# Sums of two passes transposed in 32x32 squares by VectorE in place of TensorE, with 256-byte stores

## The chip, the core and the metric

The kernel runs on one core of a Trainium2 chip. The metric is device time in microseconds (us) from start to end of one execution; lower is better. The core has TensorE (matmuls and, in the profile's own row PEld, its weight loads), VectorE (DVE), ScalarE (ACT), GpSimd (POOL) and SyncE (SP, which here issues nearly all DMAs). Sixteen DMA engines move data between DRAM and the on-chip memory SBUF; matmul results land in PSUM.

## The reference

Three layers follow each other: a linear attention over 4 batches, 8 heads, 576 positions of 64 numbers, normalised by its root mean square, which gives 2304 rows of 512; a feed-forward layer; and a mixture of four experts, all of them applied to all rows. Everything is float32:

```
kv = einsum('bhsd,bhse->bhde', k, v);  o = einsum('bhsd,bhde->bhse', q, kv)
x = (o / sqrt(mean(o * o, -1) + 1e-06) * g_norm)      # as 2304 x 512
h = x @ w_in                                          # 512 x 2048
x = (h * clip(h + 3, 0, 6) / 6) @ w_out               # 2048 x 512
p = domain_probs / (domain_probs.sum(-1) + 1e-09)     # 2304 x 4
for e in range(4):                                    # w1[e] 512 x 1024, w2[e] 1024 x 512
    out += p[:, e:e + 1] * (maximum(x @ w1[e], 0) @ w2[e])
```

Output row b*576 + s*9 + j belongs to batch b and to position (s, j) of its sequence, s from 0 to 63 and j from 0 to 8.

## The kernel before

All products are in f32 split in a high and a low part (three matmuls each). The first layer keeps its activations transposed (features on partitions, rows on the free axis); so do the experts.

The experts run in three passes of 768 rows. A pass has eight groups (g), each of two blocks of 256 hidden features; a two-by-two scheme with seven products in place of eight is used for both matrices. `front` makes the seven first products of a block (`product`, line 932, into the PSUM banks qa and qb); it reads the combined first weights `win`, two buffers, each loaded from DRAM by `load_win` (line 967) when the block two before it is done (line 1045). `back` (line 1068) makes one of the seven second products of a group in a PSUM slot (sx, sy, sz) from the combined second weights `tt` (loaded by `feed`, line 974, into four buffers, and into four more that `room` adds at the end of group 7) and adds it into the pass's sums: `acc2[th, c]`, two tiles of 128 output columns by 384 rows for each half of the rows (th) and of the 512 columns (c). VectorE does these additions (line 901) and the elementwise work of `front` and `prep`.

The sums are transposed, so a pass ends with `flush` (line 914), called four times for each of the first two passes: three times in the pass's last group (lines 1141 and 1142, after steps 2, 5 and 6), once in step 0 of the next group (line 1144). A flush makes six TensorE transposes of 128x128 into a PSUM slot, two ScalarE copies into `done` tiles in SBUF, and six stores (`store`, line 903), each of 64 rows and 256 columns, 1 KB a row. The third pass ends otherwise: its sums are transposed into PSUM with the last products (line 1169), copied to SBUF by VectorE (line 1193) and ScalarE (line 1191), and stored in rows of 2 KB from SyncE's and ScalarE's queues.

The second weights are made earlier, during the first layer, by `blocks(k, 1)` (line 667): each block of raw weights (rawt) is combined and split into high and low parts by VectorE (lines 701 and 688) and ScalarE (line 687) and written to DRAM (`dtw`, and `dwo` for the last group). A column half of 256 is contiguous there.

Order: the first stage is written out by hand; from the first layer on, a planner orders the instructions of each engine by its own costs, and each engine then runs its queue strictly in that order. SyncE's queue holds the loads of tt and win, the broadcast probabilities and the stores.

Of the kernel before, what the change touches and what calls it, by code (L numbers as in the profile page):

```python
# [11 lines left out]
AF = mybir.ActivationFunctionType  # L12
# [5 lines left out]
def kernel(  # L18
# [18 lines left out]
    nc = tc.nc  # L37
    B, H, S, D = q.shape
    NT, DM = out.shape
    E = moe2_w1.shape[0]  # L40
    P = 128
# [6 lines left out]
    CJ = S // CP  # L48
    CB = TB // CP
    HH = H // 2  # L50
# [39 lines left out]
    NG = CJ * 2  # L90
# [10 lines left out]
    ident = const.tile([P, P], F32, name="ident")  # L101
# [110 lines left out]
    half = [slice(x * D, (x + 1) * D) for x in range(2)]  # L212
# [243 lines left out]
    last = {}  # L456
# [5 lines left out]
    done = [False]  # L462
# [54 lines left out]
    with tc.manual_schedule(engines=engines):  # L517
# [88 lines left out]
        for kind, t in (("o", 1), ("i", 3), ("o", 2), ("i", 4), ("o", 3), ("o", 4)):  # L606
# [6 lines left out]
            if t == 2:  # L613
                for y in range(2):
                    nc.sync.dma_start(
                        out=dp[half[y]], in_=moe2_domain_probs.rearrange("(b s j) e -> s b j e", b=B, j=CJ))
# [4 lines left out]
        for y in range(2):  # L621
            h = half[y]
            for jp in range(2):
                j = slice(2 * y + jp, CJ - 1, 4)
                nc.vector.tensor_tensor(
                    out=prob[h, :B * HH].rearrange("p (b a) e -> p b a e", b=B)[:, :, 2 * jp:2 * jp + 2],
                    in0=dp[h, :, j], in1=psum_e[h, :, j].unsqueeze(3).to_broadcast([D, B, 2, E]), op=ALU.mult)
            nc.vector.tensor_tensor(
                out=prob[h, B * HH:], in0=dp[h, y::2, CJ - 1],
                in1=psum_e[h, y::2, CJ - 1:].to_broadcast([D, 2, E]), op=ALU.mult)  # L630

    TC = DM // 2
    experts = [(e, j) for e in range(E) for j in range(FP)]
    NG = len(experts) // 2
    INPASS = [3, 5, 7, 9, 11, 13]
# [28 lines left out]

    turns = [0]

    def blocks(k, h):

        r = rawt[k, h]
        last = k - 2 * NG + 2 if h else -1  # L670

        def new():
            turns[0] += 1
            z = ring[turns[0] % len(ring)]
            if not isinstance(z, str):
                return z
            return cvp.tile([P, 2, TC], F32R, tag=z, bufs=2 if z == "r" else 1, name="tb")

        def keep(m, src, low, n=2):
            high = new()  # L680
            low = low if low is not None else new()
            hi, lo = high[:, :n], low[:, :n]
            if src is None:
                src = lo.bitcast(F32)
            elif not h:
                hi, lo = (x.rearrange("p m (c f) -> p (m c) f", c=2) for x in (hi, lo))
            nc.scalar.activation(out=hi, in_=src, func=AF.Copy)
            nc.vector.tensor_tensor(out=lo, in0=src, in1=hi.bitcast(F32), op=ALU.subtract)
            for y, x in ((0, high), (1, low)):
                if not h:  # L690
                    nc.sync.dma_start(
                        out=dwin[k][:, y, m:m + n].rearrange("p m c f -> p m (c f)"), in_=x[:, :n].bitcast(F32))
                    continue
                c = min(n, 7 - m) if m else 1
                nc.sync.dma_start(out=dtw[k // 2][:, m:m + c, k % 2, y], in_=x[:, :c].bitcast(F32))
                if last >= 0 and m < 2:
                    nc.sync.dma_start(
                        out=dwo[last][:, int(m > 0), y].rearrange("p (c d) -> p c d", c=2), in_=x.bitcast(F32))

        def sub(out, a, b, op=ALU.subtract):  # L700
            nc.vector.tensor_tensor(out=out, in0=a, in1=b, op=op)

        odd = new()
        od = odd.bitcast(F32)
        if h:
            sub(od, r[:, 1::2], r[:, 0:2])
        else:
            q = r.rearrange("p c (i f) -> p i c f", i=2)
            a11, a12, a21, a22 = (q[:, i, 2 * c:2 * c + 2] for i in range(2) for c in range(2))
            o4 = od.rearrange("p m (c f) -> p m c f", c=2)  # L710
            sub(o4[:, 0], a21, a22, ALU.add)
            sub(o4[:, 1], o4[:, 0], a11)
        yield
        even = new()
        ev = even.bitcast(F32)
        if h:
            sub(ev[:, 0], r[:, 3], od[:, 0])
            sub(ev[:, 1], r[:, 2], ev[:, 0])
        else:
            e4 = ev.rearrange("p m (c f) -> p m c f", c=2)  # L720
            sub(e4[:, 0], a11, a21)
            sub(e4[:, 1], a12, o4[:, 1])
        yield
        keep(3, None, odd)
        yield
        keep(5, None, even)
        yield
        if h:
            keep(1, r[:, 2:4], None)
        else:  # L730
            keep(0, q[:, 0], None)
        yield
        if not h:
            keep(2, a22, None, 1)
        elif last >= 0:
            keep(0, r[:, 0:2], None)
        else:
            keep(0, r[:, 0:1], None, 1)
        rawt.pop((k, h))
        load_rawt()  # L740
        yield
# [47 lines left out]
    NPASS = len(PASSES)  # L789
    NG2 = NPASS * NG  # L790

    rows = [[(BLK[k][0] + o + y) // P for h in ps for k, o, ln, _ in h for y in range(0, ln, P)] for ps in PASSES]
# [94 lines left out]
    def slot_tile(name):  # L887
        z = slots[0] % 10
        slots[0] += 1
        return (gp if z < 8 else rp).tile([P, TB], F32, tag=("gH", "gL")[z % 2] if z < 8 else "r", name=name)  # L890
# [9 lines left out]
            else:  # L900
                nc.vector.tensor_tensor(out=a, in0=ps[:, d, :TH], in1=a, op=ALU.add)  # L901

    def store(n, src, cols, last=False):
        for y in range(2):
            if n < B * HH:
                b, a = divmod(n, HH)
                j = 4 * (a % 2) + a // 2 + 2 * y
            else:
                b, j = 2 * (n - B * HH) + y, CJ - 1
            queue = nc.scalar if y and last else nc.sync  # L910
            queue.dma_start(
                out=out.rearrange("(b s j) d -> b j s d", b=B, j=CJ)[b, j][:, cols], in_=src[half[y]])

    def flush(p, th, c, slot):

        part = acc2.pop((th, c))
        for i in range(3):
            for d in range(2):
                nc.tensor.transpose(  # L919
                    slot[:, i // 2, ((i % 2) * 2 + d) * P:((i % 2) * 2 + d + 1) * P], part[d][:, i * P:(i + 1) * P], ident)  # L920
        for i0, n in ((0, 2), (2, 1)):
            t = slot_tile("done")
            nc.scalar.activation(out=t[:, :n * TC], in_=slot[:, i0 // 2, :n * TC], func=AF.Copy)
            for i in range(n):
                store(rows[p][3 * th + i0 + i], t[:, i * TC:(i + 1) * TC], slice(c * TC, (c + 1) * TC))

    def product(k, bank, m, first):
        n = 0
# [192 lines left out]
    for g in range(NG2 - 1):  # L1121
        nxt = ahead + front(g + 1, 1)
        if (g + 2) % NG == 0 and g + 2 < NG2:
            b = build((g + 2) // NG)
            bld = {2: "5-", 4: "6-", 7: 1, 9: 6, 10: 2, 12: 5, 13: "7-", 15: 7, 16: 3, 17: "4-", 18: 4}
        else:
            bld = {z - 14: m for z, m in bld.items() if z > 13}
        ci = convert_in(2 * g + 3, *halves) if 2 * g + 3 in INPASS else iter(())
        for s in range(7):
            if s < 5:  # L1130
                prep(g, s + 2)
            back(g, s)
            for z in BEHIND[s]:
                nxt[z]()
                if z in bld:
                    b[bld[z]]()
                if z % 2:
                    next(ci, None)
            if g % 2 and s == 3:
                load_probs(g // 2 + 2)  # L1140
            if g % NG == NG - 1 and s in (2, 5, 6):
                flush(g // NG, *((0, 0), (1, 1), (1, 0))[s - 4 if s > 4 else 0], sz if s == 6 else sx)
            if g % NG == 0 and g and s == 0:
                flush(g // NG - 1, 0, 1, sz)
            if s == 5 and g + 1 < NG2 - 1:
                prep(g + 1, 0)
        if g == NG - 1:
            for _ in range(2):
                room(accp, "acc", 2)
        if g + 1 < NG2 - 1:  # L1150
            ahead = front(g + 2, 0)
            ahead[0]()
            prep(g + 1, 1)

    g = NG2 - 1
# [20 lines left out]
    for z, (jj, i, f) in enumerate(order):  # L1176
        if i not in [w[1] for w in order[:z]]:
            turn_back(i)
        last = i not in [w[1] for w in order[z + 1:]]
        t, o = divmod(i * P, TH)  # L1180
        for m, (sy_, ty) in enumerate(((0, 0), (0, 1), (1, 0))):
            nc.tensor.matmul(  # L1182
                ps[i], lhsT=hs[t, f][:, sy_, jj, o:o + P], rhs=wl[jj][:, f, ty],
                start=False, stop=last and m == 2, skip_group_check=True)
        if not last:
            continue
        r = slot_tile("done")
        for y in range(2):
            cols = slice(y * TC, (y + 1) * TC)
            if y:  # L1190
                nc.scalar.activation(out=r[:, cols], in_=ps[i][:, cols], func=AF.Copy)
            else:
                nc.vector.tensor_copy(out=r[:, cols], in_=ps[i][:, cols])
        store(rows[NPASS - 1][i], r, slice(0, DM), True)


# [28 lines left out]
```

## Time and profile before

| | |
|---|---|
| median of 3 runs | 1172.46 us (1172.0 to 1173.09) |
| profiled execution | 1172.47 us, span 1170.7 us, granted clock 0.999 |
| TensorE busy | 1157.8 us (99%) |
| VectorE busy | 914.8 us (78%) |
| ScalarE busy | 515.2 us (44%) |
| flush, TensorE transposes | 48, 6.5 us busy in all |
| flush, ScalarE copies | 16 |
| flush, stores | 48 of 64 KB, on SyncE's queue |

Busy time is the time in which an engine worked on an instruction; the span is the time from the first to the last instruction. The DMA share is the mean busy share of the sixteen DMA engines. A DMA row's duration is what SyncE spent to issue it; landing is when the data had arrived.

### The profile page before, as it was taken

How to read it: one execution, taken by the hardware profiler on the slowest of the kernel's cores; microseconds unless marked ns; L12 is line 12 of the kernel's file. 1: busy time of each engine (PE TensorE's matmuls, PEld its weight loads, DVE VectorE, ACT ScalarE, POOL GpSimd, SP SyncE). 2: the span in 40 equal slices, each digit the busy share in tenths (PEclk: the TensorE clock that was granted, in tenths of full speed). 3: DMA queues.
4: the chain of work that ended last, by engine and by line, in shares of the span. 5: the costliest groups of instructions: out<-in, count | busy, mean ns of one | idle time of the engine just before them, and what ended most of it. 6: DMA issues, size and time to landing. Idle time of an engine off the chain costs nothing.

```text
span 1170.7 us, 19129 instructions
## 1 busy us (share of the span) xinstructions
PE 1157.8 (99%) x7351; PEld 1082.2 (92%) x7351; DVE 914.8 (78%) x1602; ACT 515.2 (44%) x907; POOL 7.6 (1%) x15
## 2 busy tenths in 40 slices
PE   8999999999999999999999999999999999999998
PEld 6788888888888889999999999999999999999996
DVE  5889999977897854788888896777778867777773
ACT  6877555644555532433333444333334443333321
POOL 1100000000000000000000000000000000000000
PEclk9999999999999999999999999999999999999999
DMA  8723267488599552587878789777777887777821
GB/s 313 248 76 115 87 229 282 137 272 262 179 345 379 211 193 94 201 286 272 283 273 295 271 301 327 262 261 268 253 268 252 282 299 273 252 266 252 289 80 54
DMA packets 117219, 279.24 MB, mean 239 GB/s; under 512 B 10176, under 2 KB 69640, under 8 KB 110728
## 3 DMA queue, kind: packets, MB, share of 16 engines
q1 hardware_dynamic: 116644, 277.24, 69.1%
q8 instruction: 58, 0.95, 0.3%
q10 hardware_dynamic: 484, 0.79, 0.2%
q14 instruction: 33, 0.27, 0.1%
HBM read 212.41 MB, written 65.57 MB: 237 GB/s over the span
## 4 chain that ended last, share of the span: by engine, by line
PE 93%; DVE 3%; DMA 2%; ACT 1%; issue 0%; ACTq 0%; SPq 0%; DVEq 0%
PE slot L1078 29%; PE po L402 16%; PE qa L932 15%; PE qb L932 15%; PE ph L367 5%; PE ph L368 5%; PE ph L369 5%; PE slot L1182 1%; DMA kin<-in_k_dram 1%; DMA vin<-in_v_dram 1%; DMA qin<-in_q_dram 1%; DVE xl L323 1%; PE slot L919 0%; PE kvp L254 0%; PE zp L500 0%
## 5 line engine op out<-in xcount | busy, mean ns | idle before, releaser
L1078 PE MATMUL slot<-so,tt 128*128 128x384 f32 x1932 | 362.2, 334 | 0.0
L1078 PEld LDWEIGHTS slot<-so,tt 128*128 128x128 f32 x1932 | 337.0, 188 | 0.0
L932 PE MATMUL qa<-xs,win 128*128 128x384 f32 x1008 | 202.7, 335 | 0.2 <-ACT qa L1016 0.2
L932 PE MATMUL qb<-xs,win 128*128 128x384 f32 x1008 | 201.9, 334 | 0.0
L402 PE MATMUL po<-gH,w 128*128 128x512 f32 (+1 forms) x632 | 191.0, 368 | 0.2 <-ACT gH L383 0.2
L901 DVE TENSOR_TENSOR acc<-slot,acc 128x384 f32<-128x384 f32 x252 | 128.6, 551 | 63.3 <-PE slot L1078 63.1
L932 PEld LDWEIGHTS qa<-xs,win 128*128 128x128 f32 x1008 | 176.9, 188 | 0.9 <-ACT qa L1016 0.5
L932 PEld LDWEIGHTS qb<-xs,win 128*128 128x128 f32 x1008 | 176.9, 188 | 0.3 <-DVE ar L1011 0.2
L813 ACT ACTIVATE so<-ar 128x768 fp32r<-128x768 f32 x142 | 119.4, 844 | 99.3 <-PE slot L1078 52.9
L814 DVE TENSOR_TENSOR so<-ar,so 128x768 fp32r<-128x768 f32 x142 | 133.9, 953 | 25.8 <-ACT so L813 24.6
L402 PEld LDWEIGHTS po<-gH,w 128*128 128x128 f32 x632 | 115.6, 188 | 20.4 <-ACT gH L383 0.6
L367 PE MATMUL ph<-xh,w 128*128 128x512 f32 (+1 forms) x320 | 118.6, 371 | 0.1
L368 PE MATMUL ph<-xl,w 128*128 128x512 f32 (+1 forms) x320 | 117.9, 368 | 0.0
L369 PE MATMUL ph<-xh,w 128*128 128x512 f32 (+1 forms) x320 | 117.8, 368 | 0.0
L402 PE MATMUL po<-gL,w 128*128 128x512 f32 (+1 forms) x316 | 116.4, 368 | 0.0
L380 ACT ACTIVATE r<-ph,three 128x512 f32<-128x512 f32 (+1 forms) x80 | 51.1, 639 | 57.2 <-PE ph L369 56.4
L381 DVE SCALAR_TENSOR_TENSOR r<-r,ph 128x512 f32<-128x512 f32 (+1 forms) x80 | 50.4, 630 | 30.1 <-ACT r L380 29.7
L367 PEld LDWEIGHTS ph<-xh,w 128*128 128x128 f32 x320 | 60.3, 188 | 10.9 <-DVE r L381 0.5
L369 PEld LDWEIGHTS ph<-xh,w 128*128 128x128 f32 x320 | 60.3, 188 | 10.0
L368 PEld LDWEIGHTS ph<-xl,w 128*128 128x128 f32 x320 | 60.3, 188 | 9.9
L402 PEld LDWEIGHTS po<-gL,w 128*128 128x128 f32 x316 | 59.6, 189 | 9.9 <-DVE gL L384 0.2
L1058 DVE TENSOR_TENSOR ar<-ar 128x768 f32<-128x768 f32 x69 | 65.7, 952 | 0.6
(173 smaller groups left out, 1181.4 us busy)
## 6 DMA issues: line engine op xcount, KB each, us to landing
tt<-dtw SPq DMA_DIRECT2D x161, 512.0 KB, 4.8
win<-dwin SPq DMA_DIRECT2D x40, 1792.0 KB, 7.7
dtw<-tb SPq DMA_DIRECT2D x74, 256.0 KB, 4.9
dwin<-win SPq DMA_DIRECT2D x8, 1792.0 KB, 9.2
rawt<-in_moe_w_dram SPq DMA_DIRECT2D x24, 512.0 KB, 4.5
dwin<-tb SPq DMA_DIRECT2D x38, 256.0 KB, 3.4
raw<-in_moe_w_in_dram SPq DMA_DIRECT2D x14, 512.0 KB, 3.8
raw<-in_moe_w_out_dram SPq DMA_DIRECT2D x14, 512.0 KB, 3.5
```

The costliest lines, as they stand in the source:

```text
L367: nc.tensor.matmul(ph, lhsT=w[:, 0, c, :], rhs=xH[t][:, c, :], start=(c == 0), stop=False)
L368: nc.tensor.matmul(ph, lhsT=w[:, 0, c, :], rhs=xL[t][:, c, :], start=False, stop=False)
L369: nc.tensor.matmul(ph, lhsT=w[:, 1, c, :], rhs=xH[t][:, c, :], start=False, stop=(c == KD - 1))
L380: lambda: nc.scalar.activation(out=r, in_=ph, func=AF.Relu, bias=three[:, 0:1]),
L381: lambda: nc.vector.scalar_tensor_tensor(out=r, in0=r, scalar=6.0, in1=ph, op0=ALU.min, op1=ALU.mult),
L402: nc.tensor.matmul(po_t[u, t][o], lhsT=lhsT, rhs=rhs, start=(f == 0 and m == 0), stop=(f == UF[u] - 1 and m == 2))
L813: nc.scalar.activation(out=dst[0], in_=src, func=AF.Copy)
L814: nc.vector.tensor_tensor(out=dst[1], in0=src, in1=dst[0].bitcast(F32), op=ALU.subtract)
L901: nc.vector.tensor_tensor(out=a, in0=ps[:, d, :TH], in1=a, op=ALU.add)
L932: nc.tensor.matmul(bank, lhsT=w[:, wy, AOP[m], c], rhs=xs[m][:, xy, c], start=first and n == 0, stop=n == 5, skip_group_check=True)
L1058: nc.vector.tensor_tensor(out=dst, in0=a, in1=b, op=op)
L1078: nc.tensor.matmul(slot[:, d, :TH], lhsT=t[:, jj, ty, d * P:(d + 1) * P], rhs=o[:, sy_, jj], start=fresh and m == 0, stop=m == 5, skip_gro ...
```

## The change

The order of the second weights' output columns is changed: within a half of 256, the even columns come first, then the odd ones (`apart`, and the rearranged raw tile in `blocks`). So the two tiles of `acc2[th, c]` hold the even and the odd columns. `flush` lets VectorE transpose each tile in 32x32 squares into a `done` tile and puts even and odd results side by side: then a partition holds, for each of its output rows, 64 neighbouring columns, 256 bytes. A store takes 32 rows by 256 columns from all 128 partitions, so a flush has twelve stores in place of six, all on SyncE's queue. The last pass's copies put even and odd columns back in their places.

```diff
     def blocks(k, h):
         r = rawt[k, h]
+        if h:
+            r = r.rearrange("p c (m d) -> p c d m", d=2)
...
+            if h and src.shape[-1] == P:
+                hi, lo = apart(hi), apart(lo)
...
-            sub(od, r[:, 1::2], r[:, 0:2])
+            sub(apart(od), r[:, 1::2], r[:, 0:2])
...
-    def flush(p, th, c, slot):
+    def flush(p, th, c):
 
         part = acc2.pop((th, c))
-        for i in range(3):
+        for i0, n in ((0, 2), (2, 1)):
+            t = slot_tile("done").rearrange("p (b j d) -> p b j d", d=2, j=QP)
             for d in range(2):
-                nc.tensor.transpose(
-                    slot[:, i // 2, ((i % 2) * 2 + d) * P:((i % 2) * 2 + d + 1) * P], part[d][:, i * P:(i + 1) * P], ident)
-        for i0, n in ((0, 2), (2, 1)):
-            t = slot_tile("done")
-            nc.scalar.activation(out=t[:, :n * TC], in_=slot[:, i0 // 2, :n * TC], func=AF.Copy)
+                nc.vector.transpose(
+                    out=t[:, :n * P // QP, :, d],
+                    in_=part[d][:, i0 * P:(i0 + n) * P].rearrange("p (b j) -> p b j", j=QP))
             for i in range(n):
-                store(rows[p][3 * th + i0 + i], t[:, i * TC:(i + 1) * TC], slice(c * TC, (c + 1) * TC))
+                m = rows[p][3 * th + i0 + i]
+                for y in range(2):
+                    for z in range(2):
+                        nc.sync.dma_start(
+                            out=place(m, y)[z * QP:(z + 1) * QP, c * TC:(c + 1) * TC].rearrange(
+                                "i (a f) -> a i f", a=P // QP),
+                            in_=t[:, 4 * i + 2 * y + z].rearrange("p j d -> p (j d)"))
...
+            o = r[:, cols].rearrange("p (m d) -> p d m", d=2)
+            z = ps[i][:, cols].rearrange("p (d m) -> p d m", d=2)
             if y:
-                nc.scalar.activation(out=r[:, cols], in_=ps[i][:, cols], func=AF.Copy)
+                nc.scalar.activation(out=o, in_=z, func=AF.Copy)
             else:
-                nc.vector.tensor_copy(out=r[:, cols], in_=ps[i][:, cols])
+                nc.vector.tensor_copy(out=o, in_=z)
```

`QP` is 32, `P` 128, `TC` 256. `place(n, y)` gives the 64 output rows of half y of tile n, as `store` computed them before.

## Rows read from the trace of the kernel before

**Rows 1.** Page, part 1: busy us, share of the span, instructions of each engine.
```profile
PE 1157.8 (99%) x7351; PEld 1082.2 (92%) x7351; DVE 914.8 (78%) x1602; ACT 515.2 (44%) x907; POOL 7.6 (1%) x15
```

**Rows 2.** Busy time by stretch (us, engines, clock, DMA share, GB/s).
```profile
684.00:700.00 16.00, 16.00 (x96) 15.97 (x95) 15.42 (x28) 4.78 (x8) 0.00 (x0) 1.00 0.91 303
700.00:712.00 12.00, 12.00 (x78) 11.90 (x77) 9.67 (x14) 6.52 (x13) 0.00 (x0) 1.00 0.83 282
...
230.00:395.00 165.00, 165.00 (x774) 138.40 (x773) 133.90 (x250) 86.31 (x155) 0.00 (x0) 1.00 0.86 291
```

**Rows 3.** Timeline of the weight loads, 699 to 703.5 us (start, duration, line, tile, count).
```profile
699.18 1.05 PEld L932 LDWEIGHTS qb<-xs,win 128*128 128x128 f32 x6
700.22 0.75 PEld L919 LDWEIGHTS slot<-ident,acc 128*128 128x128 f32 x6
700.94 2.06 PEld L1078 LDWEIGHTS slot<-so,tt 128*128 128x128 f32 x12
```

**Rows 4.** VectorE: its timeline from 698.88 us, and its line 1193 grouped.
```profile
698.88 1.02 DVE L901 TENSOR_TENSOR acc<-slot,acc 128x384 f32<-128x384 f32 x2
...
L1193 DVE COPY done<-slot 128x256 f32<-128x256 f32 x6 | 2.6, 425 | 13.1 <-PE slot L1182 13.1
```

**Rows 5.** Timeline of SyncE's DMA issues, first pass end (x is the count).
```profile
689.66 0.32 SPq L967 DMA_DIRECT2D win<-dwin  x1
...
698.90 1.37 SPq L974 DMA_DIRECT2D tt<-dtw  x2
...
706.27 0.40 SPq L967 DMA_DIRECT2D win<-dwin  x1
707.06 3.70 SPq L911 DMA_DIRECT2D out_dram<-done  x6
710.86 0.54 SPq L974 DMA_DIRECT2D tt<-dtw  x1
...
714.41 0.80 SPq L974 DMA_DIRECT2D tt<-dtw  x2
...
720.86 0.38 SPq L967 DMA_DIRECT2D win<-dwin  x1
```

**Rows 6.** The same at the second pass end.
```profile
925.37 0.32 SPq L967 DMA_DIRECT2D win<-dwin  x1
...
956.03 0.32 SPq L967 DMA_DIRECT2D win<-dwin  x1
```

**Rows 7.** Line 967 (win loads): issue to landing of those at 689.66, 706.27, 720.86.
```profile
DMA to landing us min/median/max: 9.2/9.2/9.2
...
DMA to landing us min/median/max: 8.1/8.1/8.1
...
DMA to landing us min/median/max: 9.4/9.4/9.4
```

**Rows 8.** TensorE's timeline where the loads of 720.86 and 956.03 are first used.
```profile
735.73 1.20 PE L932 MATMUL qa<-xs,win 128*128 128x384 f32 x6
...
971.43 1.20 PE L932 MATMUL qa<-xs,win 128*128 128x384 f32 x6
```

**Rows 9.** Lines 911 and 615: issues on SyncE, ns min/median/max, first and last start.
```profile
L911 SPq DMA_DIRECT2D out_dram<-done x54: 466/587/1176, 690.1 to 1166.8; - x54
...
L615 SPq DMA_DIRECT2D dp<-in_moe_domain_probs_dram x2: 618/684/749, 81.9 to 82.7; - x2
```

**Rows 10.** DMA packets: queue 1 in 85 to 91 us, and all in 1160 to 1171.
```profile
q1 hardware_dynamic: 838, 0.57, 33.1%
...
DMA packets 960, 1.57 MB, mean 143 GB/s; under 512 B 192, under 2 KB 192, under 8 KB 960
```

**Rows 11.** VectorE in 150 to 400 us, line 181 grouped.
```profile
L181 DVE SCALAR_TENSOR_TENSOR a<-raw,x 128x512 uint32<-128x512 uint32 x14 | 9.6, 687 | 0.1
```

**Rows 12.** TensorE's timeline at the start.
```profile
1.45 3.78 PE L500 MATMUL zp<-zero 128*128 128x512 f32 x8 [1.45 <-DVE zero L496]
...
7.27 1.17 PE L500 MATMUL zp<-zero 128*128 128x512 f32 x4
```

More of the change, by code (lines that the diff above doesn't have):

```diff
@@ L632 @@
     TC = DM // 2
+    QP = 32
     experts = [(e, j) for e in range(E) for j in range(FP)]
@@ L665, with apart @@
     turns = [0]
+    def apart(t):
+        return t.rearrange("p c (d m) -> p c d m", d=2)
     def blocks(k, h):
         r = rawt[k, h]
+        if h:
+            r = r.rearrange("p c (m d) -> p c d m", d=2)
         last = k - 2 * NG + 2 if h else -1
@@ L716, in blocks @@
         if h:
+            od, ev = apart(od), apart(ev)
             sub(ev[:, 0], r[:, 3], od[:, 0])
@@ L901, in add_out, with place, store @@
                 nc.vector.tensor_tensor(out=a, in0=ps[:, d, :TH], in1=a, op=ALU.add)
-    def store(n, src, cols, last=False):
-        for y in range(2):
[L905 to L912, printed above, removed]
-    def flush(p, th, c, slot):
+    def place(n, y):
+        if n < B * HH:
+            b, a = divmod(n, HH)
+            j = 4 * (a % 2) + a // 2 + 2 * y
+        else:
+            b, j = 2 * (n - B * HH) + y, CJ - 1
+        return out.rearrange("(b s j) d -> b j s d", b=B, j=CJ)[b, j]
+    def store(n, src):
+        for y in range(2):
+            queue = nc.scalar if y else nc.sync
+            queue.dma_start(out=place(n, y), in_=src[half[y]])
+    def flush(p, th, c):
         part = acc2.pop((th, c))
-        for i in range(3):
+        for i0, n in ((0, 2), (2, 1)):
+            t = slot_tile("done").rearrange("p (b j d) -> p b j d", d=2, j=QP)
             for d in range(2):
-                nc.tensor.transpose(
-                    slot[:, i // 2, ((i % 2) * 2 + d) * P:((i % 2) * 2 + d + 1) * P], part[d][:, i * P:(i + 1) * P], ident)
-        for i0, n in ((0, 2), (2, 1)):
-            t = slot_tile("done")
-            nc.scalar.activation(out=t[:, :n * TC], in_=slot[:, i0 // 2, :n * TC], func=AF.Copy)
-            for i in range(n):
-                store(rows[p][3 * th + i0 + i], t[:, i * TC:(i + 1) * TC], slice(c * TC, (c + 1) * TC))
+                nc.vector.transpose(
+                    out=t[:, :n * P // QP, :, d],
+                    in_=part[d][:, i0 * P:(i0 + n) * P].rearrange("p (b j) -> p b j", j=QP))
+            for i in range(n):
+                m = rows[p][3 * th + i0 + i]
[5 more added lines that the diff above has]
+                            in_=t[:, 4 * i + 2 * y + z].rearrange("p j d -> p (j d)"))
     def product(k, bank, m, first):
@@ L1141 @@
             if g % NG == NG - 1 and s in (2, 5, 6):
-                flush(g // NG, *((0, 0), (1, 1), (1, 0))[s - 4 if s > 4 else 0], sz if s == 6 else sx)
+                flush(g // NG, *((0, 0), (1, 1), (1, 0))[s - 4 if s > 4 else 0])
             if g % NG == 0 and g and s == 0:
-                flush(g // NG - 1, 0, 1, sz)
+                flush(g // NG - 1, 0, 1)
             if s == 5 and g + 1 < NG2 - 1:
@@ L1189 @@
             cols = slice(y * TC, (y + 1) * TC)
+            o = r[:, cols].rearrange("p (m d) -> p d m", d=2)
+            z = ps[i][:, cols].rearrange("p (d m) -> p d m", d=2)
             if y:
-                nc.scalar.activation(out=r[:, cols], in_=ps[i][:, cols], func=AF.Copy)
+                nc.scalar.activation(out=o, in_=z, func=AF.Copy)
             else:
-                nc.vector.tensor_copy(out=r[:, cols], in_=ps[i][:, cols])
-        store(rows[NPASS - 1][i], r, slice(0, DM), True)
+                nc.vector.tensor_copy(out=o, in_=z)
+        store(rows[NPASS - 1][i], r)
 _INS = ['q', 'k', 'v', 'g_norm', 'moe_w_in', 'moe_w_out', 'moe2_domain_probs', 'moe2_w1', 'moe2_w2']
```

## The prediction

> **What bounds the kernel now.** I read the page's busy shares first. TensorE is busy 99% of a span of 1170.7 us [rows 1]; the profiled execution took 1172.47 us, 1.8 more than its span, and the median of the three runs is 1172.46, so sums on its rows need no scaling. The busy shares by stretch, read next around the first four flushes (684 to 712 us), show TensorE at 16.00 of 16 and 12.00 of 12 us, VectorE at 15.42 and 9.67, ScalarE at 4.78 and 6.52, and the 16 DMA engines at 0.91 and 0.83 [rows 2]. So every TensorE instruction removed is worth its time as long as nothing it needs is late. What could be late is read from SyncE's order of DMAs [rows 5, 6], the time to landing [rows 7] and the places where TensorE first uses what was loaded [rows 8].
>
> **What is removed.** Each of eight flushes (lines 914 to 925) has six TensorE transposes. In the weight loads, which set the pace here, the six begin at 700.22 and the matmuls behind them at 700.94: 0.72 us [rows 3]. The twelve loads behind then take 2.06 us; the six in front take 1.05, so twelve would be 2.10, and 0.04 comes off: 0.68 us a flush, 5.4 us for eight. With nothing late that gives 1167.0. The first flush's transposes also fill a pause in a product (line 1039) that waits for VectorE; other matmuls of the same step can fill it, so nothing is charged (0.7 us a pass if they can't). The sixteen ScalarE copies (line 923) go too: nothing, because ScalarE has more than half of these stretches free [rows 2].
>
> **What VectorE takes on.** Each flush gets four transposes, 768 columns in all. The trace has no VectorE transpose. The nearest rows are two additions of 128x384 in 1.02 us and a copy of 128x256 in 0.425 [rows 4]: 1.0 to 1.3 us a flush. The lower bound is half of that, the upper one four times that. VectorE has 0.58 us free in 684 to 700, with one flush, and 2.33 in 700 to 712, with two [rows 2], so it falls behind by 0.4 to 1 us. TensorE may wait that long, but such a wait is covered by the later one below, because it only brings TensorE later to a place where it waits anyhow. I take 0; without that cover it costs 1 to 2 us. The Trainium skill (page "VectorE: DVE Perf Modes", section "The three transpose paths") gives 311 ns for a 128x128 square of two-byte numbers; an estimate by it is six squares or 1.9 us a flush, and no run here shows it.
>
> **The second weights and the last pass.** The weight blocks read every second column. VectorE already reads such columns at line 181, 512 of them in 687 ns [rows 11], and plain ones come to the same by rows 4 (1.02 us x 512/768 = 0.68): 0. Were two strided operands dearer, VectorE has 31 us free of 165 there [rows 2]. The twelve last copies write every second column: nearest is the plain copy, 0.425 us [rows 4]; 0, at most one copy more (0.4 us) behind the last matmul.
>
> **The stores.** This is the step that decides. A flush issues six DMAs now, all on SyncE's queue, and twelve after the change, of 128 runs of 256 B each: 48 a pass end in place of 24. The loads of experts' weights (tt, line 974; win, line 967) are behind them in that queue. What a store costs in issue: now six take 3.70 us [rows 5], 0.62 each with the gap; their own duration has a median of 587 ns [rows 9]. The new pattern is not in the trace. Below lies the tt load, two in 0.80 us [rows 5]: 0.40. Above lies the DMA with the shortest runs, dp, at 684 ns [rows 9]: 0.72 with a gap. I take 0.62, the nearest in kind (the same destination, in bursts).
>
> A second limit stands in the same rows. Behind the win load of 706.27 come six stores and one tt load at 710.86, and then nothing until 714.41 [rows 5], when the load has landed (8.1 us, so 714.4) [rows 7]. The load of 689.66 lands 9.2 us later, at 698.9, and the next DMA starts at 698.90. So SyncE has at most eight DMAs under way, and a load of win holds up the eighth behind it.
>
> The first pass end, step by step. At 698.9 the load of 689.66 has landed and seven of the first twelve stores are out. Five more take 3.1 us (702.0), three tt loads at 0.40 1.2 (703.2), the second flush's twelve 7.4 (710.6), a tt load 0.4. The win load of 706.27 is issued at 711.0. Seven stores follow; then SyncE waits for its landing (8.1: 719.1). Five stores (722.2), three tt loads (723.4), the fourth flush's twelve (730.8), two tt loads (731.6). Now the win load that was issued at 720.86: 10.7 us later. It lands after 8.1 to 9.4 us [rows 7], at 739.7 to 741.0. Its first product stood at 735.73 [rows 8]; TensorE, 4 x 0.68 earlier, is there at 733.0 and waits some 7 us. Against the old schedule the pass end is 4.6 us later: the saved 2.7 us are gone in the wait. In the second pass the load of 925.37 [rows 6], at 9.4 us as well, lands at 934.8; the same steps (3.1, 1.2, 7.4, 0.4, then 8.1, 3.1, 0.4, 7.4, 0.8) bring the load of 956.03 to 966.7 and its landing to 974.8 to 976.1, where its product stood at 971.43: 4.0 us later. The tt loads have less to fear, because extra buffers are filled at the first pass end.
>
> After a long wait TensorE starts slower: its first eight products of zeros took 3.78 us, 0.47 each, four later ones 1.17, 0.29 [rows 12]. That is 1.4 us for each wait. Sum: 1172.5 + 4.6 + 4.0 + 2.8 = 1183.9, so **1184 us**. In each chain are 34 stores, so 0.1 us of issue price moves the result by 6.8 us: 0.72 gives 1191, 0.40 no wait at all and 1167 to 1168.
>
> **Rivals.** *A, few engines.* A new store's DRAM side is four strips of 32 rows, where all stores so far begin with 64 rows or more. If the four strips are what is dealt out, a store runs on four of 16 engines, 32 packets on each. A packet there costs 14 to 38 ns: in 85 to 91 us 838 packets of 0.57 MB took 33.1% of 96 engine-us [rows 10], 38 ns each at 680 B, and 256/680 of that is 14. Four flushes are 1536 packets, 21.5 us at 14 ns and 27.6 at 18. From 684 to 712 these engines have 3.5 us free [rows 2] and get 5 back from the old stores (24 stores, four packets of 1 KB each, 0.057 us by bytes). So loads land 13 to 19 us later at each pass end, of which 4 are to spare (the load of 720.86 landed at 730.3 and was used at 735.73): 9 to 15 later twice, and 2.8 for the two waits, 1193 to 1205, more if packets are dearer. For it: the shape of the store. Against it: nothing in the trace runs on fewer engines; the last twelve stores left 192 packets under 512 B, 16 each [rows 10]. The Trainium skill (page "DMA: Bandwidth & Descriptors", section "Why a DMA increments its semaphore by 16 and not by 1") has a rule for this: the number of engines is the largest up to 16 that divides the slowest dimension of both sides, here 128 and 4, so four. By that rule A is what happens; the 16 small packets a store agree with it for 64 rows, and no row tests it for four.
>
> *B, faster.* The win loads are issued ahead of the waiting stores, or a store costs 0.43 us or less. Then nothing is late and 5.4 us are kept: 1167 to 1169. For it: SyncE's order is made by a planner, which does move some tt loads ahead. Against it: the last flush (line 1144) stands in step 0 of its group and the win load (line 1045) in step 2, so the stores come first. It decides at 34 stores x 0.43 us.
>
> *C, no difference.* The issue price lies between 0.44 and 0.50, and wait and saving cancel: 1170.1 to 1174.8.
>
> *D, VectorE becomes the bound.* At four times the price (4.2 us a flush) it would be late by 3.6 us in 684 to 700 and 6.1 in 700 to 712, 19 us for both pass ends less 5.4: 1186. Against it: nothing in rows 4 moves a 4-byte column that slowly.
>
> **Chances.** Forecast 0.43 (its own range 1175 to 1193), A 0.24, B 0.21, C 0.09, D 0.03. A measurement of this kernel can't tell less than about 0.2% (2.3 us) from no change. Slower: forecast, A and D, 0.70. Same: C, 0.09. Faster: B, 0.21. The range runs from B's lower end, 1167, to just over A's, 1210; left out are dearer packets in A and little else.
>
> **What would show it.** Right, if TensorE has two new waits of 5 to 9 us for a load of win, near 733 and 970, the store line has 96 issues of about 0.6 us, and the load now at 720.86 starts near 731. VectorE's 32 transposes should be at 0.3 to 0.45 us. A shows in stores with four small packets each and in tt and win loads that land over 12 us after issue. Wrong, if TensorE's row has no wait there (B), or if its waits name VectorE (D).

## Result and profile after

The changed kernel takes 1182.94 us (median of 6 runs, 1180.78 to 1186.77), the kernel before 1172.78 beside it: a ratio of 1.0088, 95% interval 1.0071 to 1.0104. The forecast was 1184 us, slower. The profiled execution took 1182.05 us, its span is 9.5 us longer than before.

The page of after, parts 1 and 2 (its DMA line: packets, volume, how many are small), stands beside [rows 1]:

```profile
PE 1158.8 (98%) x7303; PEld 1080.4 (92%) x7303; DVE 921.8 (78%) x1634; ACT 508.1 (43%) x891; POOL 7.6 (1%) x15
...
DMA packets 126051, 279.23 MB, mean 237 GB/s; under 512 B 22080, under 2 KB 78472, under 8 KB 119560
```

TensorE has 48 instructions fewer and is busy 1.0 us longer; its idle time (span less busy) went from 12.9 to 21.4 us. So what it lost is idle time and slow matmuls, not work. SyncE's DMAs at the first pass end (start, duration, line, tile, count), against [rows 5]:

```profile
689.33 0.32 SPq L984 DMA_DIRECT2D win<-dwin  x1
691.07 12.87 SPq L939 DMA_DIRECT2D out_dram<-done  x12
704.04 1.36 SPq L991 DMA_DIRECT2D tt<-dtw  x3
705.50 9.70 SPq L939 DMA_DIRECT2D out_dram<-done  x12
...
715.81 0.38 SPq L984 DMA_DIRECT2D win<-dwin  x1
716.28 12.20 SPq L939 DMA_DIRECT2D out_dram<-done  x12
...
730.04 9.46 SPq L939 DMA_DIRECT2D out_dram<-done  x12
...
740.58 0.38 SPq L984 DMA_DIRECT2D win<-dwin  x1
```

A flush's twelve stores take 9.5 to 12.9 us where six took 3.7 at 707.06. The load of win that started at 720.86 starts at 740.58, and the three tt loads behind the first flush, of which the first went out at 694.38 and two at 698.90, go out from 704.04 on. TensorE's waits from 690 to 770 us, where before had none (waiting tile and line, what it waited for: us in all, times, longest):

```profile
PE slot L1095 <- DMA tt<-dtw: 3.2, 1, 3.2
PE slot L1095 <- ACT so L822: 1.7, 1, 1.7
PE slot L1095 <- DVE so L823: 0.6, 1, 0.6
PE qa L949 <- DMA win<-dwin: 0.4, 1, 0.4
PE qb L949 <- ACT qb L1033: 0.2, 1, 0.2
```

At the second pass end the load of win that started at 956.03 [rows 6] starts at 977.40. TensorE's waits there, from 940 to 1020 us, where before again had none:

```profile
PE slot L1095 <- ACT so L822: 1.7, 1, 1.7
PE slot L1095 <- DMA tt<-dtw: 0.7, 1, 0.7
PE qb L949 <- ACT qb L1033: 0.4, 1, 0.4
```

So of 8.8 us of waits at both pass ends 4.3 are for a load, nearly all of it for tt, and 4.5 are for operands from ScalarE and VectorE.

TensorE's timeline at the first pass end (in brackets the wait in front):

```profile
707.96 3.90 PE L1095 MATMUL slot<-so,tt 128*128 128x384 f32 x12 [3.23 <-DMA tt<-dtw]
...
737.88 2.24 PE L1095 MATMUL slot<-so,tt 128*128 128x384 f32 x12
741.82 0.44 PE L1095 MATMUL slot<-so,tt 128*128 128x384 f32 x1 [1.69 <-ACT so L822]
742.81 6.34 PE L1095 MATMUL slot<-so,tt 128*128 128x384 f32 x35 [0.55 <-DVE so L823]
749.55 1.31 PE L949 MATMUL qa<-xs,win 128*128 128x384 f32 x6 [0.40 <-DMA win<-dwin]
```

The twelve matmuls of a second product (line 1095) take 2.24 us at 737.88. At 707.96 they take 3.90, behind a wait of 3.23 us for the tt load of 704.04. In [rows 2] the granted clock of 700 to 712 us was 1.00, 2.4 GHz; in after it is 0.86 on average: 1.00 from 704 to 708 us and 0.58 from 708 to 712, so it fell to the lower level of 1.2 GHz right behind that wait:

```profile
700.00:712.00 12.00, 8.77 (x42) 8.45 (x41) 8.50 (x17) 1.42 (x3) 0.00 (x0) 0.86 0.55 167
```

VectorE's transposes and the stores' issues (ns min/median/max), for which [rows 4, 9] stood in:

```profile
L939 SPq DMA_DIRECT2D out_dram<-done x96: 536/537/3907, 691.1 to 975.7; - x96
L932 DVE STREAM_TRANSPOSE done<-acc x32: 269/355/440, 689.8 to 952.6; 128x256 f32<-128x256 f32 x16, 128x128 f32<-128x128 f32 x16
```

### The profile page after: what moved, and what is told of

It is laid out like the page before. It is cut to its first block, busy times and chain, and to the rows that moved or that the text cites. A ratio compares the mean times of both kernels' runs of the same rounds, so it can differ in the third digit from the quotient of the medians.

```text
span 1180.2 us, 19134 instructions
## 1 busy us (share of the span) xinstructions
PE 1158.8 (98%) x7303; PEld 1080.4 (92%) x7303; DVE 921.8 (78%) x1634; ACT 508.1 (43%) x891; POOL 7.6 (1%) x15
## 4 chain that ended last, share of the span: by engine, by line
PE 90%; DMA 4%; DVE 2%; SPq 2%; ACT 1%; issue 1%; ACTq 0%; DVEq 0%
PE slot L1095 27%; PE po L402 16%; PE qa L949 14%; PE qb L949 14%; PE ph L367 5%; PE ph L369 5%; PE ph L368 5%; SPq L939 2%; PE slot L1199 1%; DMA vin<-in_v_dram 1%; DMA kin<-in_k_dram 1%; DMA win<-dwin 1%; DMA qin<-in_q_dram 1%; DMA tt<-dtw 1%; DVE xl L323 1%
```

## Experiments

In all of them "shift" is how much later than before, against its own start of group 6, TensorE begins the last step of group 22, read from the starts of line 1078 (or the line that it became); in before these are 646.50 and 1141.99 us. It holds both pass ends and the groups between, and nothing of the stages ahead. After the change it is +9.55: 6.83 at the first pass end, 2.72 at the second.

| kernel | us (median) | ratio to before, 95% | shift, us |
|---|---|---|---|
| after | 1182.94 | 1.0071 to 1.0104 | +9.55 |
| a_oldstores | 1167.30 | 0.9950 to 0.9978 | -4.33 |
| b_256_16 | 1181.80 | 1.0068 to 1.0093 | +7.98 |
| b_256_4 | 1185.53 | 1.0102 to 1.0134 | +12.83 |
| a_sixteen | 1181.12 | 1.0064 to 1.0089 | +7.82 |
| b_12_1k | 1181.11 | 1.0062 to 1.0089 | +7.76 |
| b_6_256 | 1177.57 | 1.0026 to 1.0051 | +4.39 |
| a_act | 1220.24 | 1.0383 to 1.0417 | +45.06 |
| a_pool | 1326.37 | 1.1292 to 1.1323 | +152.34 |
| a_win_pool | 1191.68 | 1.0128 to 1.0165 | +10.68 |
| a_win_act | 1207.38 | 1.0268 to 1.0316 | +18.79 |
| a_half | 1189.74 | 1.0112 to 1.0153 | +8.68 |
| a_spread | 1168.94 | 0.9952 to 0.9980 | -3.75 |

### Only the stores as before: a_oldstores

```diff
-   out=place(m, y)[z * QP:(z + 1) * QP, c * TC:(c + 1) * TC].rearrange("i (a f) -> a i f", a=P // QP),
-   in_=t[:, 4 * i + 2 * y + z].rearrange("p j d -> p (j d)"))
+   out=place(m, y)[:, c * TC:(c + 1) * TC],
+   in_=t[half[y], 4 * i:4 * i + 4].rearrange("p b j d -> p (b j d)"))
```

> The kernel after, with six flush stores of 64 rows x 1 KB in place of twelve of four strips (they write what lies in the 64 partitions, so the flushed sums land in other places of the output). VectorE's transposes, the even and odd layout and the last copies are the change's. Theories 1 and 2 (the stores cost the time, by number or by engines): only the saving of 5.4 us is left, 1166 to 1169 us. Theory 3 (VectorE's transposes or the planner's order cost the time): 1175 us or more with these stores too.

Measured: 1167.3 us, 5 us below before. The stores cost everything, together with the order of instructions that the planner makes around them, which is another here than in after; VectorE's transposes, the layout and the last copies cost nothing that shows. It is also the price of "with nothing late" in the prediction, 1167.0.

### Number or engines: b_256_16, b_256_4, a_sixteen

The edits are shortened from here on; branches for the last pass are left out.

```diff
 # b_256_16, in store of the kernel before (z = 0, 1)
-   out=o, in_=src[half[y]]
+   out=o.rearrange("i (x z f) -> z i x f", z=2, f=D)[z], in_=src[half[y]].rearrange("i (x z f) -> z i x f", z=2, f=D)[z]
 # b_256_4
+   out=o[z * 32:z * 32 + 32].rearrange("i (a f) -> a i f", a=4), in_=src[:, D * (2 * y + z):D * (2 * y + z + 1)]
 # a_sixteen, in flush of the kernel after (a strip a, z = 0, 1; n tiles)
+   out=o[z * QP:(z + 1) * QP, j0:j0 + 4 * n - 1:2, f:f + 2 * QP],
+   in_=t[a * QP:(a + 1) * QP, z:4 * n:2].rearrange("i q j d -> i q (j d)")
```

> The kernel before, with one edit: each flush store of 64 rows x 1 KB is cut into two, each of 64 rows x 2 runs of 256 B, so a flush has twelve stores of 128 runs of 256 B, as after the change, but the rows (64) stand outermost. TensorE's transposes stay. Theory 1, the number of stores: SyncE pays 0.54 to 0.62 us for each and has at most eight DMAs under way, so loads of win come about 10 us later at each pass end; with nothing saved on TensorE this gives 1180 to 1185 us. Theory 2, four engines: these stores run on all 16 engines (16 semaphore packets of 4 B each, 9663 + 768 small packets in all), so loads hardly move: 1171 to 1175 us. Theory 3, the order that the planner gives TensorE, not the stores: this kernel and b_256_4 have the same order on every engine, so both have the same time.

> The kernel before with the stores of the change: twelve a flush, each of four strips of 32 rows x 256 B, 128 partitions by 256 B in SBUF. TensorE's transposes stay; the stores write the sums to other places of the output, as many bytes as before. Same order on every engine as b_256_16, same number of stores, same runs of 256 B. Theory 1, the number of stores: the same as b_256_16, 1180 to 1185 us. Theory 2, four engines: the change's loss without its saving of 5.4 us, 1185 to 1190 us, 10 us or more above b_256_16; 4 small packets per store, stores that block in issue for 1 to 4 us. Theory 3, the planner's order: the same time as b_256_16.

> The kernel after, with other stores of the same 256 B runs: a store takes 32 partitions (one strip of columns), and its DRAM side is 32 rows x 4 or x 2 runs (the output rows of one or two tiles, two rows apart), rows outermost. A flush has eight stores of 128 runs and eight of 64, sixteen in place of twelve; the output is the reference's. Theory 1, the number of stores: four more stores a flush at 0.54 to 0.62 us, about 11 more in each chain, so slower than after, 1187 to 1191 us. Theory 2, four engines: all 16 engines carry each store, loads are late by the issue price alone, 1167 to 1174 us. Theory 3 (VectorE, order): about after, 1180 to 1184 us.

The DMA line of b_256_16's page, then of b_256_4's:

```profile
DMA packets 127204, 279.25 MB, mean 237 GB/s; under 512 B 23232, under 2 KB 79624, under 8 KB 120712
```

```profile
DMA packets 126052, 279.25 MB, mean 236 GB/s; under 512 B 22080, under 2 KB 78472, under 8 KB 119560
```

1152 small packets fewer is 96 stores times 12: 16 semaphore packets a store in the one, 4 in the other, so these stores do run on four engines. What that looks like: packets of SyncE's queue from 700 to 704 us, with their share of 16 engines, first before, then after:

```profile
q1 hardware_dynamic: 421, 1.20, 87.4%
```

```profile
q1 hardware_dynamic: 1001, 0.25, 27.7%
```

A queue full of these stores keeps 4.4 of 16 engines busy (27.7%) and moves a fifth of the bytes. But that is not the four engines' doing alone. In the same 4 us of b_256_16, whose stores run on 16, it is still less:

```profile
q1 hardware_dynamic: 719, 0.16, 17.5%
```

The loads are missing there too, because they stand behind the stores. What four engines cost is the difference between b_256_4 and b_256_16, whose instructions stand in the same order on every engine: 3.7 us, where theory 2 had 10 or more. The larger part, 9.4 us, comes with all 16 engines as well: twelve stores in place of six. And a_sixteen ends at 1181.1 although TensorE has 5 us less to do than in b_256_16 (1181.8): with four more stores a flush the saving is gone in waits. Of these waits at the pass ends, 7.2 us in all, only 0.8 is for a load; the rest is for ScalarE. It was neither slower than after (theory 1) nor near 1170 (theory 2): sixteen stores on 16 engines hold SyncE for 9.2 to 13.4 us a flush, about as long as twelve on four. Its time lies in the range of theory 3, VectorE or the planner's order; a_oldstores excludes VectorE, and the order comes back below.

### Price of a store, or its place in the queue: b_12_1k, b_6_256

```diff
 # b_12_1k: 32 rows of 1 KB
+   for r in (slice(D * y, D * y + 32), slice(D * y + 32, D * y + D)):
+       nc.sync.dma_start(out=o[r.start % D:r.start % D + 32], in_=src[r])
 # b_6_256: 64 rows x 4 runs of 256 B, from the first tile of the flush
+   store(rows[p][3 * th + i0 + i], wide.rearrange("p (x z f) -> z p x f", z=2, f=D)[i], ...)
```

> The kernel before with each flush store cut into two of 32 rows x 1 KB: twelve stores a flush on 16 engines, each of 32 runs of 1 KB. Same order on TensorE and VectorE as b_256_16, same number of stores, larger runs. Number of stores as the cause: 1179 to 1183 us, as b_256_16 (1181.8), with stores that cost SyncE about 0.6 us each. Run size as the cause (128 runs of 256 B a store): 1171 to 1175 us, with stores cheaper than 0.6 us or gone sooner.

> The kernel before with six stores a flush as before, but each of 64 rows x 4 runs of 256 B (the source is four pieces of a wide tile, so the flushed sums land in other places of the output). Number of stores as the cause: 1171 to 1175 us. Run size as the cause: 1178 to 1183 us, since as many runs of 256 B are written as in b_256_16.

SyncE's DMAs in b_12_1k:

```profile
690.05 10.66 SPq L911 DMA_DIRECT2D out_dram<-done  x12
...
702.22 7.34 SPq L911 DMA_DIRECT2D out_dram<-done  x12
...
710.12 0.37 SPq L967 DMA_DIRECT2D win<-dwin  x1
710.59 11.09 SPq L911 DMA_DIRECT2D out_dram<-done  x12
...
723.19 7.18 SPq L911 DMA_DIRECT2D out_dram<-done  x12
...
731.40 0.38 SPq L967 DMA_DIRECT2D win<-dwin  x1
```

A store's own issue is at 0.42 us now (median 419 ns, 605 in b_256_16), by the prediction's sum cheap enough for no loss at all; yet a flush's twelve take 7.2 to 11.1 us, because the eighth DMA behind a load, of win or tt, stands until that load has landed (behind win: seven stores are out at 693.0, the next starts at 698.2; the load of 689.64 took 8.5). So the number alone brings the load of win to 731.40, 10.5 us later than in [rows 5], through the eight places, and to the forecast (731.6). The time is that of b_256_16.

But TensorE doesn't wait for this load, nor for any other. All its waits in b_12_1k from 600 us on are these, and at the pass ends of b_256_16 they are the same:

```profile
PE slot L1078 <- ACT so L813: 4.0, 4, 1.7
PE qb L932 <- ACT qb L1016: 0.4, 1, 0.4
```

So a second cause is at work. TensorE's timeline in b_12_1k:

```profile
735.71 2.24 PE L1078 MATMUL slot<-so,tt 128*128 128x384 f32 x12
739.64 0.44 PE L1078 MATMUL slot<-so,tt 128*128 128x384 f32 x1 [1.69 <-ACT so L813]
...
748.00 1.20 PE L932 MATMUL qa<-xs,win 128*128 128x384 f32 x6
```

The load of win of 731.40 had landed at 739.5 (8.1 us), but its first product stands at 748.00, behind a row of second products of which the one at 739.64 waits 1.69 us for ScalarE's operand. The planner had put the products there: it makes the order of TensorE out of the stores and loads that it is given, and all three kernels with twelve stores of before's tiles have that order. So in b_12_1k and b_256_16 the time is lost in the planner's order: 4.4 us in waits for ScalarE, and most of the rest in matmuls at the lower clock behind them. An estimate of what before's order would have lost in b_12_1k at this pass end: its product stood at 735.73 and the load landed at 739.5, so some 3.8 us in a wait for win. In b_6_256 the order is plainest: its load of win starts at 721.04 (720.86 in [rows 5]), lands at 730.8, and the product that stood at 735.73 in [rows 8] stands at 742.44, with the same wait of 1.69 us at 739.78. No wait of TensorE at its pass ends is for a load, so what 1177.6 us (between the two ranges expected) has above before is the planner's order and not late loads. Before's order with the new stores wasn't tried: the order follows from them.

### Other queues: a_act, a_pool, a_win_pool, a_win_act

```diff
 # a_act, a_pool: the stores of after
-   nc.sync.dma_start(
+   nc.scalar.dma_start(      # a_act
+   nc.gpsimd.dma_start(      # a_pool
 # a_win_pool, a_win_act: load_win of after
-   nc.sync.dma_start(out=win[k].bitcast(F32), in_=dwin[k % (2 * NG)])
+   nc.gpsimd.dma_start(out=win[k].bitcast(F32), in_=dwin[k % (2 * NG)])      # nc.scalar in a_win_act
```

> The kernel after with the twelve flush stores (four strips, four engines) issued from ScalarE's queue in place of SyncE's. SyncE's queue as the cause (number and issue price, loads behind the stores): loads start as before, 1167 to 1171 us, if ScalarE's 96 issues at 0.5 to 0.6 us (some 7 us a flush while it has half its time free) delay none of its copies; where they do, 1172 to 1178. Four engines as the cause: loads still share them with the stores and land late, 1174 to 1182 us.

> The kernel after with the twelve flush stores issued from GpSimd's queue, which has next to nothing else to do (7.6 us busy). SyncE's queue as the cause: 1167 to 1170 us, the saving of 5 us in full. Four engines as the cause: 1172 to 1182 us, as with ScalarE's queue. What a store costs GpSimd to issue is not in any trace so far; since nothing waits behind it there, 1 or 2 us each would not show in the time.

> The kernel after with the loads of win issued from GpSimd's queue in place of SyncE's; stores (twelve a flush, four strips) and tt loads stay on SyncE's. If the time was lost because win loads stand behind stores in SyncE's queue and take up one of its eight places for 8 to 9 us: the two pass ends lose nothing for win, and only tt loads are still behind stores, 1167 to 1173 us. If it was lost on the four engines: win loads start early but land late, after 12 us or more while stores run, 1175 to 1182 us. What may spoil it: in a_pool GpSimd spent some 2.8 us on a store of 128 runs; a win load has 128 rows of 14 KB, and GpSimd has nothing else to do.

> The kernel after with the loads of win issued from ScalarE's queue, stores and tt loads on SyncE's. Same question as a_win_pool with the other queue: 1167 to 1173 us if SyncE's order is the cause, 1175 to 1182 us if the four engines are. What may spoil it: ScalarE waits at the issue until the win buffer is free, and its copies and operands stand behind; 24 loads at up to 1 us give 0 to 24 us, as in a_act where ScalarE's operands waited behind stores.

All four missed. ScalarE's timeline in a_act:

```profile
691.45 10.63 ACTq L939 DMA_DIRECT2D out_dram<-done  x12
702.18 0.84 ACT L822 ACTIVATE so<-ar 128x768 fp32r<-128x768 f32 x1 [10.32 <-DMA tt<-dtw]
```

Twelve stores hold ScalarE's queue for 10.63 us, and ScalarE stands idle for 10.32 us ahead of the operand of line 822 behind them, on which TensorE waits (4.4 us): the stall moved to an engine that has more behind it (the releaser in the row is inferred; the queue itself was busy with the stores). In a_pool GpSimd starts a store only when the one before has landed (692.20, landed at 698.7, then 699.04; later mostly 2.5 to 2.8 us apart), so the done tiles come free late. GpSimd's gaps between stores, and ScalarE's waits for the tiles:

```profile
POOL out_dram L939 <- issue: 262.6, 92, 6.8
```

```profile
ACT acc L908 <- DMA out_dram<-done: 82.2, 3, 48.7
```

That nothing waits behind a store there was wrong: the next pass's sums wait for the tiles that it reads. In a_win_pool no load of win is in SyncE's queue, and still the twelve stores of the first two flushes take 11.3 and 13.7 us, with a load of win under way from GpSimd's; the third flush's, at 728.00 with none under way, take 7.6. So the load need not be in the same queue to hold the stores up: their four engines carry it too. The tt loads stay behind the stores, and TensorE waits 6.5 us for two of them. (9.5 us more were lost ahead of group 6, in a stretch that the edit reorders as well; ScalarE's queue in a_win_act lost 19.05 there.)

### Fewer and longer stores, spread: a_half, a_spread

```diff
 # a_half: columns by fours; both halves in one tile, 128 runs of 512 B a store
+   r = r.rearrange("p (f e) x -> p f (e x)", f=2).rearrange("p f (m c d) -> p f c d m", c=2, d=2)
+   out=place(m, y)[z * QP:(z + 1) * QP].rearrange("i (a f) -> a i f", a=P // QP), in_=...   # 4 a tile
 # a_spread: columns in runs of 32; the stores of one tile a step
-   ....rearrange("p f (m c d) -> p f c d m", c=2, d=2)
+   ....rearrange("p f (a c d m) -> p f c d a m", c=2, d=2, m=QP)
+   if g % NG == 0 and g and s < 5:
+       put(g // NG - 1, *((1, 1), (1, 2), (0, 0), (0, 1), (0, 2))[s])
```

> The kernel after, carried one step further: the second weights' columns are dealt out by fours (column 4m + 2c + d to half c, tile d), both halves' transposes go into one tile, and a store has 128 runs of 512 B, still in four strips on four engines. A pass end has 24 stores in place of 48, as many as before the change; VectorE has 48 transposes of 128x128 (281 ns each in the trace of after, 13.5 us in all); one more tile holds a sum, and flushes come in two bursts, at step 6 and at step 0. The output is the reference's. If the number of stores decides: 1166 to 1171 us, below both kernels, since a_oldstores with as many stores took 1167.3. If four engines decide as well: half of the backlog is left, 1170 to 1177 us. If the bursts of VectorE or a late buffer decide: 1175 us or more, with TensorE's waits on VectorE.

> The kernel of a_half with two edits. The 128 columns that a strip writes side by side are dealt out in runs of 32 (column 128a + 64c + 32d + j), so no operand reads every fourth column; and the stores are no longer sent in two bursts of 12: four (one tile) follow step 6 of the pass's last group and each of the steps 0 to 4 of the next group, with loads of tt and win between them. 24 stores a pass end of 128 runs of 512 B on four engines; the output is the reference's. If bursts of stores ahead of loads are what costs the time: no load of win or tt is late at a pass end, the 5 us of TensorE's transposes are kept, 1166 to 1171 us, below both kernels. If four engines cost the time however the stores are spread: 1173 to 1180 us, with loads that land 12 us or more after issue. If the layout costs VectorE in the stage of the second weights, as the 7.5 us that a_half lost before its first pass end: 1172 us or more, and all of it before the first flush.

a_half has before's number of stores and takes 1189.7. 7.5 us of it are lost ahead of the first flush, where VectorE reads every fourth column (a_half, then after, grouped by form: busy us, mean ns):

```profile
L709 DVE TENSOR_TENSOR tb<-rawt 128x512 f32<-128x512 f32 x12 | 12.9, 1074 | 2.3 <-DMA dtw<-tb 2.3
```

```profile
L709 DVE TENSOR_TENSOR tb<-rawt 128x512 f32<-128x512 f32 x12 | 8.2, 683 | 2.4 <-DMA rawt<-in_moe_w_dram 2.4
```

That is the third theory's reason, in a stage where it wasn't looked for: TensorE waits 5.9 us for VectorE between 100 and 640 us, where after has no such wait. At the pass ends it waits 8.8 us for win and not for VectorE. 8.7 us are lost there, in bursts of eight and twelve stores on four engines around a load of win:

```profile
711.39 0.33 SPq L997 DMA_DIRECT2D win<-dwin  x1
711.81 11.25 SPq L953 DMA_DIRECT2D out_dram<-acc  x8
...
725.01 11.74 SPq L953 DMA_DIRECT2D out_dram<-acc  x12
...
738.02 0.38 SPq L997 DMA_DIRECT2D win<-dwin  x1
```

With the stores spread and runs of 32, a_spread takes 1168.94 us, 0.34% below before (0.20 to 0.48) and 14 below after. SyncE's DMAs there, a tile's four stores at a time:

```profile
705.31 0.33 SPq L1005 DMA_DIRECT2D win<-dwin  x1
...
709.17 5.39 SPq L962 DMA_DIRECT2D out_dram<-acc  x4
714.66 3.64 SPq L1012 DMA_DIRECT2D tt<-dtw  x1
718.40 3.01 SPq L962 DMA_DIRECT2D out_dram<-acc  x4
...
723.20 0.38 SPq L1005 DMA_DIRECT2D win<-dwin  x1
723.67 5.67 SPq L962 DMA_DIRECT2D out_dram<-acc  x4
```

Its stores still run on four engines and still stop in issue (5.39 us for four at 709.17), but each time only four stand ahead of a load. The load of 723.20 is 2.3 us later than in [rows 5], and only one wait of 1.7 us for win is left. Two edits were made at once: 7.50 less 1.42 us of the difference lies ahead of the first flush and belongs to the layout; 12.4 us lie at the pass ends, by the shifts.

## Why the prediction was right, and where not

**Bound by TensorE, each late load counts:** the first is right: the trace of before has no TensorE wait from 690 to 770 us, that of after five kinds. The second is not, because the order of products is another in after: a load of win that started 19.7 us later (740.58 for 720.86) cost a wait of 0.4 us.

**5.4 us of TensorE removed:** 5.2 by the spans of a_oldstores and before (1165.5 and 1170.7), of which 4.3 lie at the pass ends by the shift. The transposes on VectorE are at 281 and 431 ns, 10.7 us in 32, so 1.3 us a flush, at the upper end of the 1.0 to 1.3 taken, and covered. Stride 2 costs nothing (683 and 686 ns for the same operation after and before). What was put at 0 shows no cost in a_oldstores.

**The stores delay the loads in SyncE's queue:** right for the loads, and the eight places are shown by b_12_1k. But the term was mis-sized. The issue price was taken at 0.62 us and came to 0.54; the load was forecast for 731.6 and started at 740.58, because a flush takes 9.5 to 12.9 us, not 7.4. From the load of 689 to this one the forecast had 41.9 us; b_12_1k took 41.8, b_256_16 46.5, after 51.3. So 4.6 of the 9.3 us too much also come with 16 engines, where a store starts 0.65 us after the last one and the queue stands behind tt loads and stores as well as behind win; of the other 4.7, 3.3 come with four engines (b_256_4 took 49.8), where the stores stop in issue for up to 3.9 us each, also where fewer than eight DMAs are out; the last 1.4 lie between b_256_4 and after and weren't traced further. And that the lateness of these loads is what TensorE loses is not shown: b_12_1k and b_256_16 lose 8 us with no wait for a load, through the planner's order.

**Rival A, few engines (0.24):** its condition holds, its price does not: 3.7 us in all between b_256_16 and b_256_4, where A had loads 9 to 15 us late at each pass end. The Trainium skill (page "DMA: Bandwidth & Descriptors", section "Why a DMA increments its semaphore by 16 and not by 1") says that the engines are the largest number up to 16 that divides the slowest dimension of both sides; 4 small packets a store agree with it. A's second sign, loads of win that land over 12 us after issue, did not come: the load of 740.58 had landed by 749.5. The forecast and A are not two outcomes but two terms of one.

**Two waits of 5 to 9 us for win:** not so; this is the step that failed. TensorE waits 0.4 us for the late win load at the first pass end and not at all at the second. The prediction kept before's order of products; the planner, which is given the new stores, had moved the products of win behind second products, so the loss at the first pass end is in pieces: 3.2 us for a tt load, 1.7 for an operand, 1.1 in small waits, and 1.7 in matmuls at a lower clock (3.90 for 2.24 us). They make 7.7 us; 6.83 and the 2.7 saved make 9.5 lost in all at this end, so some 1.8 are left, spread over single matmuls. That tt loads had "less to fear" was wrong: the largest wait is one of theirs. Two errors went against each other: the load came 9 us later than forecast, and TensorE had other work in the meantime. So it is luck that 1184 and 1183 agree better than the steps do.

**Restart at a lower clock, 1.4 us a wait:** 1.66 us behind the wait of 3.23 at 707.96; almost nothing behind waits of 1.69 and 0.55 at after's first pass end. At its second (1.69 and 0.66), and in b_12_1k and b_256_16 (1.69 and 0.29), eight to ten matmuls at 320 ns in place of 173 followed, so the cost can't be read from the length of the waits alone.

**Rivals B, C, D:** b_12_1k has about B's limit of 0.43 us a store (0.42, 0.47 from start to start), and its time is not B's: the loads were late through the eight places without the price, and the order was the planner's new one. C needed a price of 0.44 to 0.50 us, and it was 0.54. D is excluded by a_oldstores.

What stays open: how much the new stores would cost with before's order, in which TensorE would meet the late loads, and so whether the planner's order loses more than it saves. b_6_256, whose load of win at the first pass end is on time, shows 4.4 us with no wait for a load. In after the load landed just as its product stood there (a wait of 0.4 us), so no order could have used it sooner.

## What to carry to other kernels

When work moves off a full engine, count what takes its place in each queue: here 24 more DMAs a pass end cost 14.7 us of span (9.5 and the 5.2 saved), nearly three times what the transposes had: in part through loads that go out late behind a queue with eight places, in part through the order of products that a planner makes around them. So when the order is made by a planner, read the new order before counting a late load as a wait. Give a store an outermost dimension that all 16 engines can share (64 and 32 rows did here; four strips ran on four), and send stores a few at a time between the loads rather than at the end in a block: the change, done so, is 0.3% faster and not 0.9% slower. No other queue helped here: behind the stores or loads that were moved there stood something that TensorE needs, the tiles that the stores read included.

## What was not expected of the hardware

- Reading f32 columns at stride 2 costs VectorE nothing (683 ns for 128x512), at stride 4 it costs 1.6 times as much (1074 ns). A transpose of 128x128 whose output is written at stride 4 took 384 ns, at stride 2 281, in runs of 32 columns 279.
- A store on four engines keeps its queue's engine at the issue for up to 3.9 us (line 939 of after), though by its four small packets 12 of the 16 DMA engines have no part in it.
- GpSimd issues a store of 128 runs in 692 ns, but had only one under way at a time: the next of the 96 in a_pool started 2.5 us later or more, and never before the one ahead had landed.
- SyncE started none of its DMAs before the eighth ahead of it had landed: no exception in the 443 of before's trace for which a landing is recorded.
